# Retention and a mixture of experts on one core: up projections by seven half-size products instead of eight, sent between the down projections, with the attention as a chain of chunks

## The chip, the cores and the metric

One core of a Trainium2 chip. The metric is the device time of the core in microseconds (us), the median of several executions. The names in the profile: PE is the tensor engine's matmuls, PEld its weight loads, DVE VectorE, ACT ScalarE, POOL GpSimd, SP SyncE; "PEq" or "SPq" is the sequencer of an engine, where DMAs are issued. "PEclk" is the clock granted to PE, in tenths of full speed; "half clock" below means that the record of it reads 0.5.

## The reference

```python
def _attn_ref(q, k, v):                       # (8, 8, 576, 64): batches, heads, tokens, width
    scores = scale * np.matmul(q, k.transpose(0, 1, 3, 2))
    gamma = 1.0 - 2.0 ** (-5.0 - np.arange(H))            # one decay per head
    Dmat = np.where(rel >= 0, gamma[:, None, None] ** rel[None], 0.0)   # causal, rel = i - j
    return np.matmul(scores * Dmat[None], v)

def _moe_ref(x, domain_probs, w1, w2):        # x (4608, 512), w1 (4, 512, 1024), w2 (4, 1024, 512)
    p = domain_probs / (domain_probs.sum(-1, keepdims=True) + 1e-09)
    for e in range(E):
        h = np.maximum(x @ w1[e], 0.0)        # up projection
        out += p[:, e:e + 1] * (h @ w2[e])    # down projection
    return out
```

The attention's output, heads side by side, is the `x` of the mixture. The 4608 tokens are worked on in 9 tiles of 512, and each tile meets all four experts: 36 pairs of tile and expert.

## The kernel before

Attention and mixture run in one program. While tile t is multiplied, batch t+1's attention is slipped in between the groups of matmuls. The decay is split into a gain on k and a gain on q; whole chunks of 128 tokens leave a state (k transposed times v) behind for the chunks after them. A batch has 576 tokens: four chunks and a remainder of 64. The parts that matter here:

```python
# one pair: 32 up matmuls of 512 columns, ReLU on ACT, then 32 down matmuls
def up(ph, e, fc, ts):
    for dc in range(NDC):                                             # NDC = 4
        nc.tensor.matmul(ph[:, ts], lhsT=w1_sb[e][:, dc, fc * 128:(fc + 1) * 128],
                         rhs=xT[:, dc, n0 + ts.start:n0 + ts.stop], start=(dc == 0), stop=(dc == NDC - 1))
# ups(e): for fc in range(8): up(...); nc.scalar.activation(hT[:, fc, :], ph, Relu); yield
# downs(e): for ns in range(4): 8 matmuls into po, then
#           acc = po * p (ACT, first expert) or acc += po * p (DVE); the last expert stores acc
# ... (cut)
# batches 2 to 7: what goes in after which group of the tile before (32 up and 16 down groups)
at(19 if nt == 1 else 17, lambda: state["A"].S([0, 1]))               # scores of two head pairs
at(24, lambda: state["A"].Srem(), lambda: state["A"].O_values([0, 1]),
   lambda: state["A"].kv_all(), lambda: state["A"].kv_sum(), lambda: state["A"].Srem_mask())
at(28, lambda: state["A"].O_states([0, 1]))
at(30, lambda: state["A"].S([2, 3]))
at(34, lambda: state["A"].O_values([2, 3], rem=True), lambda: state["A"].O_states([2, 3], rem=True))
```

The score matmuls use 64 rows of the array (two heads side by side), the value and kv matmuls 64 columns; the state matmuls and all projections use the full 128x128 array. Tile 0 and the first part of tile 1 ("the head" below) run with batches 0 and 1, whose q and k are transposed by PE; from batch 2 on the DMA transposes.

## Time and profile before

| | before |
|---|---|
| time, median | 561.0 us (560.97 to 561.14 in the first three runs) |
| span of the profiled run, granted clock | 557.7 us, 0.999 |
| PE busy | 546.5 us |
| DVE, ACT, POOL busy | 166.9, 217.5, 118.6 us |

The page of the kernel before: busy time of each engine with its share of the span, then busy tenths in 40 slices of the span.

```profile
span 557.7 us, 8401 instructions
## 1 busy us (share of the span) xinstructions
PE 546.5 (98%) x3462; PEld 261.4 (47%) x3462; DVE 166.9 (30%) x288; ACT 217.5 (39%) x371; POOL 118.6 (21%) x203
...
PE   7999999899999999999999999999999999999997
...
PEclk9999999999999999999999999999999999999999
```

The chain of work that ended last, in order of time (start, length, what):

```profile
139.20 6.91 PE po L552 x32
146.11 6.91 PE ph L518 x32
153.01 6.91 PE po L552 x32
```

32 matmuls of 512 columns in 6.91 us are 216 ns each, one behind the other. The timeline of PE shows the head's landmarks (start, length, operation, output<-inputs, tile, count); the later comparison rests on these starts. The first line is the first up projection, the second batch 1's first scores, the third and fourth the start of tile 1's first up projections and the transposes of batch 1's remainder within them, and the last the first down projection of tile 1, where the head ends.

```profile
17.88 0.61 PE L518 MATMUL ph<-xT,wt 128*128 128x256 bf16 x4
...
65.92 0.40 PE L319 MATMUL s<-qkT 64*128 64x128 bf16 x8
...
83.13 2.77 PE L518 MATMUL ph<-xT,wt 128*128 128x384 bf16 x20
85.83 0.29 PE L266 MATMUL ptr<-ident,qrb 64*128 64x64 bf16 x4
...
90.85 7.07 PE L552 MATMUL po<-wt,hT 128*128 128x512 bf16 x32
```

And this is one piece of attention, 16 score matmuls, between projections:

```profile
239.62 1.89 PE L518 MATMUL ph<-xT,wt 128*128 128x512 bf16 x8
241.44 0.62 PE L286 MATMUL s<-qkT 64*128 64x128 bf16 x16
241.99 1.04 PE L518 MATMUL ph<-xT,wt 128*128 128x512 bf16 x4
```

How much PE time such a piece takes is read from starts: the 8 projections before it would be followed at 239.62 + 8 x 0.216 = 241.35 by the next one; it came at 241.99; so the piece cost 0.64 us (its median over the trace is 0.649). "The cost of a piece" below always means this.

### The profile page before, as it was taken

Reading aid. Unit: us, or ns where it says so; the run is one execution under the profiler, and the core shown is the slowest. Engines: PE = TensorE matmul, PEld = TensorE weight load, DVE = VectorE, ACT = ScalarE, POOL = GpSimd, SP = SyncE. Lnnn points to the kernel's source line nnn. Section 1 sums busy time; section 2 is a strip of 40 time slices with the busy share of each in tenths; the row PEclk is TensorE's granted clock in tenths of the full one; section 3 lists DMA queues with packets and bytes.
Section 4 is the critical chain, followed back from the end, with each engine's and each line's share of the span. In section 5 each row is a group of like instructions: output and inputs, shape, how many; then the busy total and the mean of one; then the engine's idle time right before and its main releaser. Section 6 shows DMA issues by size and latency. Waiting matters only on the chain.

```text
span 557.7 us, 8401 instructions
## 1 busy us (share of the span) xinstructions
PE 546.5 (98%) x3462; PEld 261.4 (47%) x3462; DVE 166.9 (30%) x288; ACT 217.5 (39%) x371; POOL 118.6 (21%) x203
## 2 busy tenths in 40 slices
PE   7999999899999999999999999999999999999997
PEld 4544444354445444544445444544454444444443
DVE  5402461253214520462035212532046202220222
ACT  6543424333353235323433334323532353335332
POOL 7701366026002420045002600260010000000000
PEclk9999999999999999999999999999999999999999
DMA  8999999491369025910595048903200100010002
GB/s 232 182 206 200 200 204 238 99 212 22 113 121 182 1 85 95 220 19 38 114 177 88 1 132 149 136 1 104 58 2 0 76 0 1 0 76 0 1 0 76
DMA packets 148805, 53.83 MB, mean 97 GB/s; under 512 B 130684, under 2 KB 143228, under 8 KB 148768
## 3 DMA queue, kind: packets, MB, share of 16 engines
q1 hardware_dynamic: 141296, 44.79, 40.2%
q0 software_dynamic: 7328, 8.39, 8.9%
q8 instruction: 27, 0.44, 0.4%
q10 hardware_dynamic: 144, 0.13, 0.1%
q14 instruction: 10, 0.08, 0.1%
HBM read 45.16 MB, written 9.44 MB: 98 GB/s over the span
## 4 chain that ended last, share of the span: by engine, by line
PE 82%; DMA 11%; SPq 3%; POOL 3%; issue 1%; DVE 0%; POOLq 0%
PE po L552 40%; PE ph L518 37%; DMA raw_v<-in_v_dram 4%; DMA wt<-in_moe_w_dram 2%; DMA raw_vr<-in_v_dram 2%; SPq L278 1%; PE o L358 1%; PE s L286 1%; DMA raw_k<-in_k_dram 1%; DMA raw_q<-in_q_dram 1%; PE o L366 1%; POOL wt L125 1%; SPq L85 1%; DMA qkT<-km 0%; SPq L91 0%
## 5 line engine op out<-in xcount | busy, mean ns | idle before, releaser
L539 ACT ACTIVATE hT<-ph 128x512 bf16<-128x512 f32 x288 | 171.9, 598 | 275.4 <-PE ph L518 275.4
L518 PE MATMUL ph<-xT,wt 128*128 128x512 bf16 (+2 forms) x1172 | 260.0, 376 | 0.0
L552 PE MATMUL po<-wt,hT 128*128 128x512 bf16 (+1 forms) x1160 | 255.9, 378 | 0.0
L552 PEld LDWEIGHTS <-hT 128*128 128x128 bf16 x1160 | 112.5, 98 | 132.9 <-DMA wt<-in_moe_w_dram 0.3
L518 PEld LDWEIGHTS <-wt 128*128 128x128 bf16 x1172 | 111.9, 98 | 127.9
L558 DVE SCALAR_TENSOR_TENSOR acc<-po,probs,acc 128x512 f32<-128x512 f32 (+1 forms) x109 | 81.3, 746 | 229.1 <-PE po L552 221.9
L293 DVE TENSOR_TENSOR sT<-s,tri 128x512 bf16<-128x512 f32 x48 | 29.8, 684 | 115.6 <-PE s L286 115.6
L556 ACT ACTIVATE acc<-po,probs 128x512 f32<-128x512 f32 x36 | 24.8, 690 | 38.2 <-PE po L552 38.2
L272 POOL COPY kbd<-qkT 64x256 bf16<-64x256 bf16 x12 | 4.8, 398 | 129.7 <-DMA qkT<-krb 129.4
L407 POOL CAST sbd<-ksum 64x256 bf16<-64x256 f32 x36 | 14.3, 398 | 83.3 <-DVE ksum L412 74.0
L239 POOL TENSOR_TENSOR km<-raw_k,gk 128x512 bf16<-128x512 f32 x28 | 29.1, 1041 | 12.5 <-DMA raw_k<-in_k_dram 10.9
L241 POOL CAST vm<-raw_v 128x512 bf16<-128x512 f32 x28 | 17.1, 612 | 41.9 <-PE o L358 35.2
L241 POOL CAST qm<-raw_q 128x512 bf16<-128x512 f32 x28 | 17.0, 608 | 3.6 <-DMA raw_q<-in_q_dram 3.2
L378 DVE TENSOR_TENSOR xT<-o,gq 128x512 bf16<-128x512 f32 x24 | 15.5, 686 | 6.0 <-PE o L366 5.5
L244 POOL TENSOR_TENSOR krb<-raw_kr,gk 64x512 bf16<-64x512 f32 x8 | 8.3, 1036 | 19.0 <-DMA raw_kr<-in_k_dram 19.0
L286 PE MATMUL s<-qkT 64*128 64x128 bf16 x192 | 7.7, 218 | 2.3 <-DMA qkT<-km 2.3
L286 PEld LDWEIGHTS <-qkT 64*128 64x128 bf16 x192 | 5.4, 94 | 7.6 <-issue 5.1
L358 PE MATMUL o<-sT,vm 128*64 128x128 bf16 x192 | 7.6, 222 | 0.0
L248 POOL CAST vbd<-raw_vr 64x256 bf16<-64x256 f32 x16 | 6.4, 398 | 3.4 <-DMA raw_vr<-in_v_dram 3.0
L358 PEld LDWEIGHTS <-vm 128*64 128x64 bf16 x192 | 5.7, 109 | 2.9 <-issue 2.5
L366 PE MATMUL o<-qkT,sbd 128*128 128x128 bf16 x72 | 6.2, 220 | 0.1
L141 PE MATMUL warm_out<-kbd 128*128 128x512 bf16 x14 | 4.9, 500 | 1.3 <-DVE kbd L136 1.3
(97 smaller groups left out, 152.2 us busy)
## 6 DMA issues: line engine op xcount, KB each, us to landing
out_dram<-acc SPq DMA_DIRECT2D x35, 256.0 KB, 2.0
raw_k<-in_k_dram SPq DMA_DIRECT2D x32, 256.0 KB, 5.1
raw_q<-in_q_dram SPq DMA_DIRECT2D x32, 256.0 KB, 5.1
raw_v<-in_v_dram SPq DMA_DIRECT2D x32, 256.0 KB, 5.2
wt<-in_moe_w_dram POOLq DMA_DIRECT2D x6, 1024.0 KB, 25.8
wt<-in_moe_w_dram POOLq DMA_DIRECT2D x4, 512.0 KB, 7.3
raw_kr<-in_k_dram SPq DMA_DIRECT2D x8, 128.0 KB, 5.1
raw_qr<-in_q_dram SPq DMA_DIRECT2D x8, 128.0 KB, 5.0
```

The costliest lines, as they stand in the source:

```text
L239: eng.tensor_tensor(o, i, gk[:, c, :].unsqueeze(2).to_broadcast([128, H, D]), op=MULT)
L241: eng.tensor_copy(o, i)
L286: nc.tensor.matmul(s[j][:, c, :], lhsT=self.qkT[r, 1, p, cs], rhs=self.qkT[r, 0, p, cs], start=True, stop=True)
L293: nc.vector.tensor_tensor(st[:, j], s[j], tri[:, :].unsqueeze(1).to_broadcast([128, NCH, C]), op=MULT)
L358: nc.tensor.matmul(o[64 * j:64 * j + 64, c * C:(c + 1) * C], lhsT=self.m["v"][:, c, 2 * p + j, :], rhs=self.sT[p][:, j, c, :], start=(c == ...
L378: nc.vector.tensor_tensor(xT[:, p, b * S:b * S + SM], o, gq[:, p, 0:SM], op=MULT)
L407: eng.tensor_copy(sbd[r, n, :, r], src[r])
L518: nc.tensor.matmul(ph[:, ts], lhsT=w1_sb[e][:, dc, fc * 128:(fc + 1) * 128], rhs=xT[:, dc, n0 + ts.start:n0 + ts.stop], start=(dc == 0), s ...
L539: nc.scalar.activation(hT[:, fc, :], ph, Relu)
L552: nc.tensor.matmul(po, lhsT=hT[:, fc, ns * 128:(ns + 1) * 128], rhs=w2_sb[e][:, fc, d:d + w], start=(fc == 0), stop=(fc == NFC - 1))
L556: nc.scalar.activation(a, po, Copy, scale=pe)
L558: nc.vector.scalar_tensor_tensor(a, po, pe, a, op0=MULT, op1=ADD)
```

## The change

Strassen's scheme (in Winograd's form) computes a 2x2 block product with seven half-size products instead of eight. Applied to an up projection (1024x512 times 512x512), it needs 7 x 8 matmuls of 256 columns where there were 32 of 512. The price is sums: of blocks of the weights, once per expert (DVE, in the head), of blocks of x, once per tile (POOL), and of products in PSUM (ACT and DVE, each half pair: a pair is done in two halves of its 1024 hidden features). To hide these the products alternate with the *down* projection of the pair before, four down matmuls to each gap between products. The attention of batches 2 to 7 becomes a chain of small tasks, at most one PE task to a gap. The head, with tile 0 and the first pair of tile 1, stays classical: 31 of the 36 pairs are fast ones. Also, q gets its gain as it is cast (before: as the attention's output left PSUM).

The core of the diff, shortened and not in the order of the file (cuts marked with `# ...`):

```diff
+    def weight_sums(e):                      # 10 DVE operations and 2 late ones per expert
+        # ... t1 = a21 + a22; t2 = t1 - a11; copies of both to bf16; a12 - t2; late: a21 = a11 - a21
+    def token_sums(nt):                      # 6 POOL operations per tile, scratch t1, t2 from pool "tmp"
+        # ... b12 - b11, b22 - t1, b22 - b12, b21 - t2, and two copies to bf16
+    def up_fast(nt, e, g, gap, window):      # one half pair
+        product(P, lambda k: w[:, k, :HF], lambda k: x[:, k, t0], start=True)
+        nc.scalar.activation(Q, P, Copy)
+        product(R_, lambda k: s[:, 0, k], lambda k: T[:, 0, k], start=True)
+        nc.scalar.activation(m5, R_, Copy)
+        window("DVE")
+        gap()
+        product(P, lambda k: s[:, 1, k], lambda k: T[:, 1, k])
+        nc.vector.tensor_tensor(R_, P, m5, op=ADD)
+        # ... four more products; hT gets ReLU(Q), ReLU(R_), ReLU(P), and P + m5 (DVE, clamped by POOL)
+        # ... (cut)
+        def gap():
+            for _ in range(4):
+                f = next(fill)               # one down matmul of the pair before
+                if f:
+                    evacuations.append(f)
+            sums(nt + 1)
+            pool(nt, 2)                      # two POOL tasks of the chain
+            chain.emit("PE", nt)             # at most one PE task of the chain
+            chain.seen.update(chain.done)
+            chain.now += 1
+        # ... (cut)
+            # the chain of a batch: scores S, kv and outputs O of the chunks, then the remainder
+            Sc(0, 0, -1 if n else 0), kv(0, 0), Sc(1, 2, 0), O(0, 3, 0), kv(1, 4), Sc(2, 5, 1), O(1, 6, 0), kv(2, 7)
+            Sc(3, 8, 2), O(2, 9, 0), kv(3, 10)
+    # ... (cut)
+    at(48, narrow, lambda: [f() for f in token_sums(1)], lambda: [a1().cast_rem(n, nc.gpsimd) for n in "kqv"])
+    sums_at(1, 17)                           # weight sums of expert 1 from group 17 of the head on, and so on
+    sums_late(1, 22)
+    sums_at(0, 23)
+    sums_at(2, 33)
+    sums_late(2, 38)
+    sums_at(3, 48)
+    sums_late(3, 53)
 # ... (cut)
-    apool = ctx.enter_context(tc.tile_pool(name="apool", bufs=6))
+    apool = ctx.enter_context(tc.tile_pool(name="apool", bufs=NSUB))        # 4 accumulators
```

## The prediction

> **What bounds the kernel now.** The tensor engine. The page has PE busy 546.5 us of a 557.7 us span; the rest mostly goes by before the first projections. In the chain of work that ended last PE holds 82%, and from 107 us on it reads "32 matmuls, 6.91 us" again and again: 216 ns per 128x512 matmul, no gaps. A tile of 512 tokens (one down projection to the same one a tile later, 226.93 to 286.37 us) takes 59.4 us: 8 x 6.91 = 55.3 of projections and 4.2 of the next batch's attention. Other engines have room (the page: DVE 30%, ACT 39%, POOL 21%); the granted clock is 0.999 (cores view). Only fewer PE cycles can help.
>
> **What is removed.** 31 of the 36 pairs of tile and expert go from 32 up matmuls of 512 columns to 7 x 8 = 56 of 256 columns. The trace has such matmuls: in the last down projection twelve in a row, each with its weight load, take 1.47 us from first start to last end (timeline); the last one lasts 0.27, so 11 starts take 1.20 us, 109 ns each. The Trainium skill, "TensorE: Matmul & The Clock Gate", section "Wait — 56ns, not 53.3ns?", gives a fixed cost of about 2.5 ns per warm matmul; 109 and 216 agree. A weight load takes 98 ns (groups), so it still hides, barely. Per pair: 56 x 0.109 = 6.10 against 6.91, 0.80 us saved; x 31 = 25 us, all on the critical path.
>
> **What is added.** Per pair, DVE gets four additions of 128x512 (estimate 0.7 us each, from the mask's 0.684), ACT four copies (0.6, as the Relu) less two Relus, POOL two clamps. Per tile, POOL gets six token sums and q's gain multiplication (1.04 us where the cast took 0.61). Estimated DVE load is 31 us of a 56 us tile, POOL 28: neither becomes the bound. The weight sums (48 DVE operations) fall into the first tile, beside evacuations with slack. Attention's matmuls stay, one piece per gap.
>
> **New waits.** Banks P, Q, R are reused within a half pair of about 6.5 us. Laid out with these durations each reuse has slack but one: the last product's Relu has four down matmuls (0.86 us, plus one matmul's 0.11) until P is written again, and needs about 0.27 + 0.6 + two semaphore steps = 1.0 us. I allow 0.05 us x 62 = 3 us. The attention chain may reach tile 2 late: 1 us, about what the old waits for transposes (2.3 us, groups) give back. The head stays within 1 us.
>
> **Sum.** 561 - 25 + 3 = 539 us. Range 532 to 547. Faster by over 2% (under 549.8): 0.92; within 2%: 0.07; slower: 0.01.
>
> **What would show it.** PE busy about 521 us; 256-column matmuls 109 ns apart inside a product; a tile period near 56.3 us; PE idle under 3 us in the fast part, ended by ACT's last Relu; DVE 45 to 50% busy; no wait for tokens at a tile's start.
>
> **What would make it wrong.** Weight loads that no longer hide: 20 ns x 1736 would cost 35 us and cancel the gain. PSUM-to-PSUM copies much slower than 0.6 us would make the P, Q, R chain PE's bound. Late tokens would show as PE idle of several us at tile starts. Output stores held up behind transposes could stall ACT, as only four accumulators are left.

The 109 ns in it were read from this line of the timeline of the kernel before, twelve matmuls of 256 columns in the last down projection:

```profile
552.64 1.47 PE L552 MATMUL po<-wt,hT 128*128 128x256 bf16 x12
```

## The result

| | before | changed |
|---|---|---|
| time, median | 560.99 us | 559.62 us (558.53 to 560.90) |
| ratio, 95% interval | | 0.9969 (0.9948 to 0.9990) |
| span of the profiled run, clock | 557.7 us, 0.999 | 558.7 us, 0.988 |
| PE busy | 546.5 us | 535.0 us |

A ratio is the mean time of a kernel's fast runs over that of the kernel before in the same rounds, so it isn't quite the ratio of the medians. The kernel before has a spread of its own: over all experiments, its 15 runs with a mean clock of 0.999 or 1.0 took 559.8 us on average, its 24 with 0.996 or 0.997 took 561.3, and 5 with 0.994 took 562.5. The traced execution is one of the first kind, so a comparison of the traces favours the kernel before by more than 1 us against the medians. The change is "the same" within 2%: 1.7 us gained where 22 were predicted. The page after:

```profile
span 558.7 us, 10485 instructions
## 1 busy us (share of the span) xinstructions
PE 535.0 (96%) x4133; PEld 334.5 (60%) x4206; DVE 266.3 (48%) x427; ACT 251.6 (45%) x450; POOL 225.9 (40%) x321
...
PE   8999876799999999999999999999999999999997
...
PEclk9999979799999999999999999999999999999999
```

PE is 11.5 us less busy, as it should be to some extent, yet the span is longer: PE is idle in slices 5 to 8 (56 to 112 us), and the granted clock drops there.

**Where the gain is.** A half pair without attention, on PE's timeline of the changed kernel (before: 13.82 / 2 = 6.91 us):

```profile
318.12 0.60 PE L583 MATMUL upP<-xT,wt 128*128 128x256 bf16 x4
318.55 0.60 PE L583 MATMUL upR<-tsum,wsum 128*128 128x256 bf16 x4
318.99 1.03 PE L519 MATMUL po<-wt,hT 128*128 128x512 bf16 x4
...
324.63 0.60 PE L583 MATMUL upP<-xT,wt 128*128 128x256 bf16 x4
```

From start to start 6.51 us: 28 x 0.109 + 16 x 0.216. Products follow each other 0.43 us apart, 4 matmuls of 109 ns. The fast matmuls do what was predicted: 31 pairs x (56 x 0.1095 - 32 x 0.2159) = -24.1 us.

**Where it went, first half: the head.** The same landmarks as before, on the changed kernel's PE timeline; a bracket is idle time of PE, with what ended it:

```profile
19.76 0.61 PE L478 MATMUL ph<-xT,wt 128*128 128x256 bf16 x4
...
72.73 0.61 PE L315 MATMUL s<-qkT 64*128 64x128 bf16 x8 [4.75 <-DVE qkT L298]
...
90.84 2.77 PE L478 MATMUL ph<-xT,wt 128*128 128x384 bf16 x20
100.42 0.39 PE L306 MATMUL ptr<-ident,qrb 64*128 64x64 bf16 x4 [6.80 <-POOL qrb L275]
...
108.37 0.60 PE L583 MATMUL upP<-xT,wt 128*128 128x256 bf16 x4
```

| landmark, start in us | before | changed | behind |
|---|---|---|---|
| first up projection | 17.88 | 19.76 | 1.9 |
| batch 1's first scores | 65.92 | 72.73 | 6.8 |
| tile 1's first up projections | 83.13 | 90.84 | 7.7 |
| transposes of batch 1's remainder | 85.83 | 100.42 | 14.6 |
| end of the head | 90.85 | 108.37 | 17.5 |

The head loses 17.5 us, 11.55 of them in two waits. The stretches-of-time view gives a mean clock of 0.89 from 60 to 91 us and 0.80 from 91 to 108.4 us: in each wait a stretch of 6.8 us at half clock begins (71.07 to 77.89 and 98.38 to 105.20 us in the clock record), in which 512-column matmuls start 427 ns apart. Of the two, 5.2 and 4.8 us lie after the wait's end; half of that, 5.0 us, is an estimate of what they cost. With the waits and the later start that is 18.4 us; less a wait of 0.92 us that only the kernel before has there (for POOL, at 71.9 us), it comes to the 17.5 lost. The Trainium skill, "TensorE: Matmul & The Clock Gate", section "HAM oscillation — how this bites in real kernels", says that an idle gap of more than some 3.4 us sends the clock to half; the trace agrees (waits of 4.75 and 6.80 us), but shorter waits did so in other runs (see the last section).

The first wait is for a copy on DVE. Its queue, on DVE's timeline of the changed kernel:

```profile
50.89 0.41 DVE L553 CAST wsum<-tmp 128x512 bf16<-128x512 f32 x1
...
68.22 1.26 DVE L553 CAST wsum<-tmp 128x512 bf16<-128x512 f32 x1
69.40 0.41 DVE L554 CAST wsum<-tmp 128x512 bf16<-128x512 f32 x1
...
70.34 2.01 DVE L556 TENSOR_TENSOR wt<-wt 128x512 bf16<-128x512 bf16 x2
72.27 0.41 DVE L298 COPY qkT<-ptc 128x512 bf16<-128x512 bf16 x1
```

On POOL's timeline:

```profile
67.72 1.48 POOL L267 TENSOR_TENSOR km<-raw_k,gk 128x512 bf16<-128x512 f32 x1
```

Expert 2's weight sums stand ahead of the copy, and they are slow there: such a cast takes 0.41 us at 50.89 and at 69.40, when POOL is idle, and 1.26 us at 68.22, when POOL multiplies k by its gain until 69.20. The Trainium skill, "SBUF — State Buffer", section "SBUF: two separate sides", has DVE and POOL share a port pair as an exclusive lock; the slow cast agrees with it, but no run here separates this from the order of the queue. The second wait is for a cast on POOL that stands behind six token sums (91.55 to 97.88), which could only start when batch 1's last tokens were there:

```profile
91.55 1.15 POOL L566 TENSOR_TENSOR tmp<-xT 128x512 f32<-128x512 bf16 x1 [15.69 <-DVE xT L233]
...
97.88 1.04 POOL L275 TENSOR_TENSOR krb<-raw_kr,gk 64x512 bf16<-64x512 f32 x1
98.88 1.48 POOL L275 TENSOR_TENSOR qrb<-raw_qr,gq 64x512 bf16<-64x512 f32 x1
```

**Second half: the attention in pieces.** A piece of 8 score matmuls in the changed kernel:

```profile
300.24 1.03 PE L519 MATMUL po<-wt,hT 128*128 128x512 bf16 x4
301.19 0.40 PE L315 MATMUL s<-qkT 64*128 64x128 bf16 x8
301.52 0.61 PE L583 MATMUL upP<-tsum,wt 128*128 128x256 bf16 x4
```

It costs 301.52 - (300.24 + 4 x 0.216) = 0.42 us, where 16 cost 0.65 before. So 8 matmuls are 0.22 us, and every piece has 0.20 us on top. Over all pieces of batches 2 to 7:

| | before | changed |
|---|---|---|
| pieces, and cost in all | 30, 27.8 us (2.5 of it waiting for a transpose) | 84, 36.0 us |
| score piece, median | 0.649 (16 matmuls) | 0.425 (8) |
| kv piece | with the value piece | 0.341 (8) |
| output piece with states | 1.242 (with the remainder) | 0.674 |
| remainder's scores, full array | with the value piece | 0.116 (4 of 64 columns) |

The remainder's scores, which use the full array, have no such surcharge: 256 columns in all for 0.116 us, where one 256-column matmul takes 0.109. The surcharge goes with the tiling: the kernel before has 24 pieces with smaller tiles in these batches, the changed one 72, and 48 x 0.217 us (the surcharge that the experiments give) is 10.4 us, where the costs differ by 36.0 - (27.8 - 2.5) = 10.7. The Trainium skill, "TensorEngine Tiling (Array Packing)", section "Key Properties", says that changing the tiling mode drains the tensor engine, without a figure. I had not looked at this page before predicting.

From the end of the head to the last down projection the kernel before takes 547.02 - 90.85 = 456.2 us. In the changed one it starts after the four down matmuls of the last gap, which begin at 547.13, so at 548.0, and 439.6 us have passed: 16.5 us gained, which is 24.1 for the products less 8.2 for the pieces, within 0.6. With 17.5 lost in the head this makes the 1.0 us by which the changed span is longer. (The medians have it 1.4 us shorter: the traced execution of the kernel before is some 1.5 us under the span of its median run, that of the changed kernel 0.8 us above.)

### The profile page after: what moved, and what is told of

It is laid out like the page before. It is cut to its first block, busy times and chain, and to the rows that moved or that the text cites. A ratio compares the mean times of both kernels' runs of the same rounds, so it can differ in the third digit from the quotient of the medians.

```text
span 558.7 us, 10485 instructions
## 1 busy us (share of the span) xinstructions
PE 535.0 (96%) x4133; PEld 334.5 (60%) x4206; DVE 266.3 (48%) x427; ACT 251.6 (45%) x450; POOL 225.9 (40%) x321
## 4 chain that ended last, share of the span: by engine, by line
PE 91%; DVE 5%; issue 1%; POOL 1%; DMA 1%; SPq 0%; POOLq 0%; DVEq 0%
PE po L519 43%; PE upP L583 20%; PE upR L583 10%; PE ph L478 5%; PE upQ L583 5%; PE oc L356 2%; PE s L315 2%; PE kvp L326 1%; PE oc L359 1%; DVE wt L556 1%; DMA raw_q<-in_q_dram 1%; DVE wsum L555 0%; PE warm_out L153 0%; DVE acc L509 0%; DVE xT L233 0%
## 5 line engine op out<-in xcount | busy, mean ns | idle before, releaser
L604 POOL TENSOR_SCALAR hT<-hT 128x512 bf16<-128x512 bf16 x62 | 38.1, 614 | 211.5 <-DVE hT L603 210.7
L595 DVE TENSOR_TENSOR upR<-upP,m 128x512 f32<-128x512 f32 x62 | 43.4, 699 | 126.9 <-PE upP L583 126.9
L583 PEld LDWEIGHTS <-wsum 128*128 128x128 bf16 x744 | 72.6, 98 | 21.1
L583 PE MATMUL upP<-tsum,wt 128*128 128x256 bf16 x496 | 74.8, 273 | 0.1
L603 DVE TENSOR_TENSOR hT<-upP,m 128x512 bf16<-128x512 f32 x62 | 42.9, 692 | 55.7 <-PE upP L583 54.2
L494 ACT ACTIVATE hT<-ph 128x512 bf16<-128x512 f32 x40 | 23.5, 597 | 41.6 <-PE ph L478 40.8
L478 PE MATMUL ph<-xT,wt 128*128 128x512 bf16 (+3 forms) x174 | 39.7, 377 | 0.6 <-issue 0.4
L583 PE MATMUL upP<-xT,wt 128*128 128x256 bf16 x248 | 37.4, 273 | 0.0
L583 PE MATMUL upQ<-xT,wt 128*128 128x256 bf16 x248 | 37.2, 273 | 0.0
L583 PE MATMUL upP<-tsum,wsum 128*128 128x256 bf16 x248 | 37.2, 273 | 0.0
```

Of the source, the lines that this page charges most:

```text
L583: nc.tensor.matmul(ps[:, l], lhsT=wa(kc)[:, f:f + 128], rhs=xa(kc), start=(start and l == 0 and kc == 0), stop=(kc == 1), skip_group_check ...
L595: nc.vector.tensor_tensor(R_, P, m5, op=ADD)
L603: nc.vector.tensor_tensor(h22, P, m5, op=ADD)
L604: nc.gpsimd.tensor_scalar(h22, h22, float("inf"), 0.0, op0=MIN, op1=MAX)
```

## The experiments

My theory was thus: the products bring their 24 us; the head's waits (called Q, for queue order, in the expectations) and changes of tiling (D) take it back. Rivals: the fast part doesn't deliver and the head doesn't matter (F); POOL's own slowness makes the waits (P); the cost of a piece belongs to each insertion, whatever its tiling (G). "Against the changed kernel" below is the difference of the two ratios to the kernel before, times 561 us, as the calls need not have run on the same chip.

### e1_sums_early: weight sums where DVE idles

```diff
-    sums_at(1, 17)
+    sums_at(1, 17, 10)
     sums_late(1, 22)
-    sums_at(0, 23)
-    sums_at(2, 33)
-    sums_late(2, 38)
+    sums_at(0, 18, 10)
+    sums_at(2, 23)
+    sums_late(2, 34)
```

> The changed kernel with the weight sums of experts 1, 0 and 2 put earlier in VectorE's program (into its idle stretch at 29 to 43 us), so that none stands ahead of the q and k copies of batch 1. Theory Q (queue order: the 4.75 us wait of the score matmuls at 68 us is a copy queued behind weight sums on VectorE): that wait goes, and so does the half-clock stretch after it; 5 to 7 us faster than the changed kernel, near 553.5; the 6.8 us wait of the remainder's transposes on POOL stays. Rival F (the fast part's 256-column matmuls do not deliver and the head does not matter): within 1 us of 559.6. Rival P (the copy is late because POOL's casts are late): the wait stays above 3 us.

552.51 us, ratio 0.9847 (0.9819 to 0.9875): 6.8 us less than the changed kernel. The wait for the copy is gone, one half-clock stretch is left of two, and the 6.80 us wait stays. Theory Q holds for the first wait; F and P fall for it.

### e2_rem_early: the remainder's casts ahead of the token sums

```diff
-    at(48, narrow, lambda: [f() for f in token_sums(1)], lambda: [a1().cast_rem(n, nc.gpsimd) for n in "kqv"])
+    at(48, narrow, lambda: [f() for f in token_sums(1)])
+    at(44, lambda: [a1().cast_rem(n, nc.gpsimd) for n in "kqv"])
```

> The changed kernel with batch 1's remainder casts on POOL put ahead of the six token sums instead of behind them. Theory Q: the transposes no longer wait (6.8 us gone there), but their copies on VectorE stand behind the weight sums of expert 3, which wait for the token sums' scratch buffers, so most of the wait moves to the remainder's score matmuls: a new PE wait of 3 to 6 us on VectorE's copy, and only 1 to 4 us faster than the changed kernel, 556 to 558. Rival P (POOL's order alone): 7 us or more faster, below 553.

559.36 us, ratio 0.9976 (0.9941 to 1.0011): no gain. The list of PE's waits has this in the place of the one removed:

```profile
PE sr L368 <- DVE kbd L290: 6.4, 1, 6.4
```

The wait moved on almost whole (6.4 of 6.8 us) to the next matmuls, whose operands DVE copies behind expert 3's weight sums, and those wait for the scratch buffers that the token sums hold, 2.79 and 2.73 us on DVE's timeline. The second of these waits:

```profile
97.02 1.52 DVE L550 TENSOR_TENSOR tmp<-tmp,wt 128x512 f32<-128x512 f32 x1 [2.73 <-POOL tsum L568]
```

The mechanism was as expected; the 1 to 4 us weren't there.

### e3_both: both, and expert 3's sums spread over the fast part

```diff
-    sums_at(3, 48)
-    sums_late(3, 53)
+    spread, late[3] = weight_sums(3)         # after the head
+    spread += late[3]
 # in gap():
+            if spread:
+                spread.pop(0)()
```

> Both moves, and expert 3's weight sums spread one per gap over the first fast pairs. Theory Q: PE's two waits in the head go (11.5 us), and with them the two half-clock stretches (estimate 3 to 4 us, from 21 matmuls of 512 columns at 427 instead of 216 ns): 543 to 547. What remains to the 539 predicted is then the attention's smaller pieces (estimate 8 us). Rival F: above 556.

550.69 us, ratio 0.9811 (0.9783 to 0.9839): 8.9 us less than the changed kernel, where 13 to 17 were expected. Both waits are gone and the head ends at 91.44 us, but twelve matmuls later stands a new one, in which a half-clock stretch begins:

```profile
98.58 0.61 PE L315 MATMUL s<-qkT 64*128 64x128 bf16 x8 [5.24 <-DMA qkT<-km]
```

It is the transpose of batch 2's first chunk. In the changed kernel PE had been late enough not to meet it.

### e4_dup: one product computed twice

```diff
         product(P, lambda k: w[:, k, :HF], lambda k: x[:, k, t0], start=True)
+        product(P, lambda k: w[:, k, :HF], lambda k: x[:, k, t0], start=True)
```

> The changed kernel with the first product of each half pair computed twice (the second start overwrites the first, the result stays right): 62 x 4 more 256-column matmuls. If PE's stream bounds the fast part and such a matmul costs 109 ns, 27 us slower than the changed kernel, 586.5 (585 to 589). If instead the chain P, Q, R through ACT and VectorE bounds it, PE has room and it costs under 10 us, below 570; if weight loads did not hide, over 32 us.

585.47 us, ratio 1.0446 (1.0407 to 1.0486), results right: 26.8 us more than the changed kernel for 62 x 4 matmuls, 108 ns each. The fast part is bound by PE's stream, and a 256-column matmul costs what the trace of before said. The chain through P, Q and R does not bound it, and the weight loads hide.

### e5_pair and e6_pair_sf: fewer pieces, and fewer changes of tiling

e5_pair sends each kv piece in one gap with the output piece before it:

```diff
-            chain.emit("PE", nt)
+            if chain.emit("PE", nt) and chain.done["PE"] % 14 in (4, 7, 10):
+                chain.emit("PE", nt, strict=False)
 # O(0, 3, 0), O(1, 6, 0), O(2, 9, 0) become O(0, 4, 0), O(1, 7, 0), O(2, 10, 0)
```

e6_pair_sf also puts the state matmuls of an output piece, which use the full array, ahead of its value matmuls:

```diff
+            for p in range(NP if c else 0):
+                nc.tensor.matmul(o[:, p, :], lhsT=sbd[:, c - 1, p, :], rhs=self.qc(0, c)[:, p],
+                                 start=(p == 0), stop=False, skip_group_check=True)
             # ... value matmuls, start=(c == 0 and p == 0)
-            # ... the state matmuls stood here
```

> The changed kernel, with each kv piece of the attention sent in the same gap as the output piece before it (18 times), so 66 insertions into the projections instead of 84; the output piece still ends with its full-array state matmuls, so for 12 of the 18 the array's tiling changes as often as before. Theory D (each change into 64-row or 64-column tiles and back costs about 0.2 us, a drain): the 12 pairs cost as much as the two pieces alone (0.674 + 0.341 = 1.0 us each), only the 6 pairs without state matmuls save 0.2 us; about 1.2 us in all, near 558.4. Rival G (each insertion costs, whatever the tiling): 18 x 0.2 = 3.6 us.

> As the run before it in this list, and the state matmuls (full array) come first in the output piece, so that its tiled part and the kv piece are neighbours. Theory D: all 18 pairs now cost about 0.2 us less than the two pieces alone (0.8 instead of 1.0 us), 3.6 us in all, near 556. Rival G: the same as the run before it.

Median costs in the two traces: a pair with states takes 1.015 us in e5_pair (0.674 + 0.341, to the last digit the two alone) and 0.787 in e6_pair_sf, where an output piece with the states first costs 0.663 alone; a pair without states, the first chunk's, takes 0.564 in both, against 0.440 + 0.341 alone. So a pair saves 0.217 us (0.663 + 0.341 - 0.787 and 0.440 + 0.341 - 0.564) exactly where it saves a change of tiling, and nothing elsewhere: theory D holds for the pieces, and G falls. But the times were 565.26 us (ratio 1.0088, 1.0059 to 1.0118) and 564.11 us (1.0065, 1.0036 to 1.0094), 5 to 7 us *more* than the changed kernel. That expectation failed. In both PE waits anew for ACT: in e6_pair_sf 6.9 us in two waits, the longer of 5.5 us (in e5_pair 6.0 and 4.9), in which a third half-clock stretch begins. On PE and, just before, on ACT in e6_pair_sf:

```profile
182.03 1.01 PE L584 MATMUL upP<-tsum,wsum 128*128 128x256 bf16 x4 [5.47 <-ACT upQ L590]
```

```profile
180.80 0.69 ACT L508 ACTIVATE acc<-po,probs 128x512 f32<-128x512 f32 x1 [6.64 <-DMA out_dram<-acc]
```

ACT waits for an accumulator whose store to memory is late; SyncE issues stores in one queue with transposes and loads. In the changed kernel the same wait is 1.86 us, and PE doesn't feel it.

### e12_pair_store: the same with stores out of SyncE's queue

```diff
-                eng.dma_start(out=out[t * 128:(t + 1) * 128, cols], in_=a)
+                stores.append(store)          # ACT issues it at the next evacuation, when acc is long done
```

> e6_pair_sf with the output stores taken out of SyncE's queue. e6_pair_sf was slower than the changed kernel although its attention took 4 us less, and I put that to ACT waiting 6.6 us for an accumulator whose store stood behind transposes. If so: the 6.9 us wait of PE for ACT goes, and the run is 3 to 4 us faster than the changed kernel, 555 to 557. If the wait was something else, it stays above 562.

554.78 us, ratio 0.9888 (0.9866 to 0.9910): 4.5 us less than the changed kernel. PE's wait for ACT is gone, the two waits of the head are as they were. So the store was the cause, and 18 saved changes are worth their 18 x 0.217 = 3.9 us, within the noise.

### e8_before_split and e13_split_scores: the kernel before with more pieces

e13 halves the score pieces; e8 does that and puts kv_all and kv_sum one group after O_values.

```diff
-            at(19 if nt == 1 else 17, lambda: state["A"].S([0, 1]))
+            at(19 if nt == 1 else 17, lambda: state["A"].S([0]))
+            at(20 if nt == 1 else 18, lambda: state["A"].S([1]))
 # and S([2, 3]) at 30 becomes S([2]) at 30 and S([3]) at 31
 # e8 alone: kv_all, kv_sum at 25 instead of at 24
```

> The kernel before, with its attention cut into smaller pieces: score matmuls of one head pair per insertion instead of two (12 more tiled pieces in the six batches), and the kv matmuls one group later than the value matmuls instead of next to them (6 more). Same matmuls, no Strassen products. Theory D: each more change of tiling costs about 0.2 us wherever it happens: 18 x 0.2 = 3.6 us slower than the kernel before, +0.6%, and in the trace an 8-matmul score piece takes 0.425 us as in the changed kernel, where the 16-matmul one took 0.649. Rival: the cost belongs to the changed kernel's gaps (semaphores, short products); then within 1 us of the kernel before.

> The kernel before, with only the score matmuls cut in two: 12 more tiled pieces in the six batches, the kv matmuls left where they were. Theory D: 12 x 0.217 = 2.6 us slower than the kernel before, +0.5% (0.3 to 0.7%), and no new wait of PE over 1 us. e8_before_split was 8.6 us slower, of which its trace gives 4 us to waits for POOL's state copies that my moving the kv matmuls had made, not to drains.

e8 took 569.79 us, ratio 1.0153 (1.0140 to 1.0166), 8.6 us more. That is more than twice what I expected. The pieces themselves are as expected (score piece 0.426 us; the two halves of the cut group 0.780 + 0.721, together 0.217 more than the 1.284 before), but the states now came late and PE waited 4.0 us for POOL's copies, in six waits; that was my edit. The clean cut, e13, took 563.68 us, ratio 1.0046 (1.0031 to 1.0062): 2.6 us more, as predicted from 12 x 0.217. So a change of tiling costs the same without any of the new scheme.

### e9_casts_early and e7_best: two runs with wrong results

Both cast batch 2's first chunks on POOL before the token sums; e7_best has e6_pair_sf's pairs too.

```diff
-    for g in range(49, 56):
+    for g in [45, 46, 47] + list(range(49, 56)):
         at(g, lambda: pool(1, 2))
```

> As e3_both, and POOL casts the first two chunks of batch 2 before the token sums of the second tile instead of behind them. Theory Q: the 5.2 us wait for the transposes, which e3_both had in the place of the two removed waits, goes with its half-clock stretch: 5.2 + about 1.5 us faster than e3_both's 550.7, 543 to 545. If another wait appears in the head, the gain is under 3 us.

> e9_casts_early and e6_pair_sf together. If waits in the head and drains add up: 3.6 us faster than e9_casts_early, 539 to 542, the time that was predicted for the change (539), and over 3% faster than the kernel before.

Their results were wrong (relative error 0.07), by my mistake: six tasks more before the end of the head let batch 2's remainder overwrite vbd and kbd, which hold the remainder's values and keys, while batch 1 still needed them. The times (554.05 and 559.64 us; PE waited 9 to 10 us for the overtaking cast of vbd) say nothing about the theories.

### e10_head_store and e11_all: the same made right

```diff
-    for g in [45, 46, 47] + list(range(49, 56)):
+    for g in (45, 46, 47, 52, 53, 54, 55):
 # and the stores as in e12_pair_store; e11_all has the pairs too
```

> e9_casts_early made right (POOL's early work limited so that it doesn't overtake batch 1's remainder) and the output stores of the fast part issued by ACT one step later, so that they no longer stand behind transposes in SyncE's queue. Theory Q: no PE wait over 2 us is left in the head; 5.2 us of wait and about 1.5 us of half clock less than e3_both (550.7): 543 to 546.

> e10_head_store with the output and kv pieces paired, state matmuls first. If the drains saved add to it: 3.6 us faster than e10_head_store, 539.5 to 542.5; the pairs must not bring back the wait of ACT for output stores that e6_pair_sf had (6.6 us).

549.22 us (ratio 0.9789, 0.9775 to 0.9804) and 545.73 us (0.9727, 0.9712 to 0.9742). The pairs save 3.5 us, as expected, and e11_all is the first that is over 2% faster than the kernel before beyond its interval (e10_head_store's reaches 0.9804). But e10_head_store missed its 543 to 546: the wait for batch 2's transposes is still there, 4.5 us (5.2 in e11_all), though the casts were early. What was late is the issue. SyncE's timeline in e11_all:

```profile
83.47 1.11 SPq L109 DMA_DIRECT2D raw_k<-in_k_dram  x1
84.62 1.09 SPq L109 DMA_DIRECT2D raw_q<-in_q_dram  x1
...
91.93 1.32 SPq L284 DMA_TRANSPOSE qkT<-qm  x1
```

Each load holds SyncE for about 1.1 us, from 72 to 90 us without a pause, and the transposes come after them in its program.

### e15_head_later and e14_all_later: the first scores five gaps later

```diff
-                        ok = (b, c) in self.begun and (not strict or self.now >= self.begun[b, c] + 5)
+                        ok = (b, c) in self.begun and (not strict or self.now >= self.begun[b, c] + (13 if (b, c) == (2, 0) else 5))
```

> e10_head_store, with the first score piece of batch 2 held back five gaps (about 8 us), so that it comes after its transposes, which SyncE issues only at 92 us because its queue is full of loads until then. If that was the last wait of the head: 4.5 us of wait and half of 6.8 us at half clock go, 7.9 us in all, and it takes 541.3 (540 to 543). If the chain of the attention gets late by it, PE waits at the second tile and the gain is under 3 us.

> e11_all with the same score piece held back: 5.2 us of wait and 3.4 us of half clock less than 545.7: 537 (535.5 to 539), 3.6 to 4 us under e15_head_later through the 18 saved changes of tiling. It would be 4.2% faster than the kernel before, the gain that the products alone were predicted to give.

545.01 us (ratio 0.9733, 0.9708 to 0.9759) and 545.23 us (0.9715, 0.9692 to 0.9738). The transposes' wait is gone, but both missed: a fourth wait came, 3.1 and 2.9 us. In e14_all_later, on PE and on POOL:

```profile
117.26 1.03 PE L528 MATMUL po<-wt,hT 128*128 128x512 bf16 x2 [2.86 <-POOL hT L613]
```

```profile
115.65 0.85 POOL L290 COPY kbd<-qkTr 64x256 bf16<-64x256 bf16 x2 [13.99 <-DMA qkTr<-krb]
116.59 0.61 POOL L613 TENSOR_SCALAR hT<-hT 128x512 bf16<-128x512 bf16 x1
```

The clamp of hT stood behind a copy that waited 14 us for another transpose that SyncE had issued late. The two kernels differ by the pairs, which were expected to save 3.6 to 4 us; the ratios differ by 1.0 us, and the intervals overlap (the runs spread over 4 us), so these two runs neither show nor refute that saving.

### e16_krem_later: that copy eight gaps later

```diff
-    (13 if (b, c) == (2, 0) else 5)
+    {(2, 0): 13, (2, NCH): 13}.get((b, c), 5)
```

> e14_all_later, with POOL's copy of batch 2's remainder keys put eight gaps later in POOL's program. In e14_all_later that copy held POOL for 14.0 us (waiting for a transpose that SyncE issues only at 113 us), the clamp of hT stood behind it, and the down projection waited 2.9 us for the clamp. If that was the last wait of the fast part's start, it goes: 2 to 4 us less than e14_all_later's 545.2, 541 to 543, with PE's only wait over 1.5 us in the trace gone and the clock at half nowhere after 20 us. If a further wait appears, it is within 1 us of 545.

540.67 us, ratio 0.9636 (0.9613 to 0.9658), results right: 4.4 us less than e14_all_later by the ratios (its range had 2 to 4), and 20.4 us less than the kernel before. Its page:

```profile
span 538.8 us, 10541 instructions
## 1 busy us (share of the span) xinstructions
PE 529.3 (98%) x4206; PEld 334.3 (62%) x4206; DVE 258.6 (48%) x427; ACT 251.3 (47%) x450; POOL 222.7 (41%) x321
...
PEclk9999999999999999999999999999999999999999
```

PE's longest wait is 1.3 us, at the start; the head ends at 90.23 us (90.85 in the kernel before) and has no half-clock stretch; the 66 insertions cost 31.2 us. All of the products' gain is there but for the pieces, which still cost more than before (31.2 against 27.8 us).

## Why the prediction was wrong

The prediction was 539 us (532 to 547), 92% for faster by over 2%; measured were 559.62.

- **Right: the bound and the products.** "Per pair ... 0.80 us saved; x 31 = 25 us, all on the critical path": 24.1 in the trace (0.78 per pair), and 26.8 us for doubling one product (e4_dup). Weight loads hide: 109.5 ns.
- **Right, with too much allowed: the P, Q, R chain.** 3 us were set aside for the last ReLU; PE doesn't wait for it in the changed kernel.
- **Wrong, the step that failed first: "The weight sums (48 DVE operations) fall into the first tile, beside evacuations with slack", and "The head stays within 1 us".** The head lost 17.5 us. I had checked that DVE has time on average; what counts is what stands ahead of what in its queue. One batch's copies, which PE needs at once, stood behind weight sums on DVE, and the remainder's casts behind token sums on POOL, and the two are also tied by shared scratch buffers (e2_rem_early). In each wait a stretch of 6.8 us at half clock began. Shown by e1_sums_early (one wait, 6.8 us) and by the sequence up to e16_krem_later.
- **Wrong: "Attention's matmuls stay, one piece per gap", taken as free.** The matmuls are the same, but 84 insertions instead of 30 cost 36.0 us instead of 27.8, 0.217 us for each change into a smaller tiling and back. Shown on the traces of e5_pair and e6_pair_sf, on time by e11_all (3.5 us against e10_head_store; e14_all_later against e15_head_later did not show it), and in the kernel before by e13_split_scores (2.6 us).
- **Seen, and not given a size: "Output stores held up behind transposes could stall ACT".** It does nothing in the changed kernel, but it cost e6_pair_sf over 5 us, and e12_pair_store removed it.
- **What was to show it:** DVE came out 48% busy, as predicted (45 to 50); PE busy was 535 us instead of 521, for the half clock and the pieces; a tile took 57.8 us on average (56.0 to 61.9, tiles 2 to 6) instead of 56.3. "The attention chain may reach tile 2 late" did not happen; PE meets no wait for tokens at a tile's start.

Why no single repair gave the gain back: behind each wait stood another resource that was just as late. Removing the DVE wait left POOL's; removing both left the transposes, late for SyncE's issue; then POOL behind a late transpose. With all four gone and 18 changes of tiling saved, the kernel takes 540.7 us, close to the 539 predicted for the change as it stood. That the two agree to 2 us is partly luck: the 3 us set aside for the ReLU were not used, and the pieces still cost 3.4 us more than before.

Open: how much of the slow DVE sums is POOL's share of the port and how much comes from the longer queue alone; and the 1.9 us by which the changed kernel starts its first projections later (19.76 against 17.88 us; 18.97 in e16_krem_later), which no run isolates.

## What to carry to other kernels

When a change trades tensor work for small operations on other engines, check for each operation that the tensor engine will wait for what stands ahead of it in its engine's queue, not how busy that engine is; and take waits away together, since the next one often stands right behind. Count the changes of the array's tiling: at 0.2 us each, many small tiled pieces between full-array matmuls cost more than a few large ones. A wait of a few us costs more than itself if the clock falls to half in it.

## What the Trainium skill lacked or had wrong

- "TensorEngine Tiling (Array Packing)", "Key Properties", says that changing the tiling mode drains the engine and gives no figure. Here it is 0.217 us for going from the full array to 64-row or 64-column tiles and back (e5_pair, e6_pair_sf, e8_before_split).
- "TensorE: Matmul & The Clock Gate", section "Back-to-back issue gap", gives about 131 ns as the sustained spacing of 512-column matmuls with a weight load each. Here it is 216 ns (6.91 us for 32), which is the same page's formula for the isolated gap; 256 columns take 109 ns.
- The same page, section "HAM oscillation — how this bites in real kernels", puts the idle gap that sends the clock to half at more than some 3.4 us. Here stretches at half clock also began in waits of 3.1 us (e15_head_later, 6.8 us at half), 2.9 (e14_all_later, 3.4 us) and 2.3 (e8_before_split and e13_split_scores, 3.4 us), while the same wait of 2.3 us in the trace of the kernel before had none. Most stretches lasted 6.8 us in the clock record, of which 3.5 to 6.1 us came after work was back.
- "DMA: Bandwidth & Descriptors", section "Issuing engines are not separate DMA queues", calls the sequencer's time to start a DMA usually small next to the DMA. Here one load of 256 KB held SyncE for about 1.1 us of the 4.8 to 5.1 us (medians) from issue to landing, one transpose for 1.2 to 2.0 us where 2.5 is the median to landing, and 18 us of loads stood ahead of the transpose that PE waited for (e11_all).
- "SBUF — State Buffer" describes the lock between DVE and POOL and names two slowdowns without the operations they belong to; it has no time for a DVE cast beside a POOL operation. Here a 128x512 cast on DVE took 0.41 us alone and 1.26 beside a 1.48 us multiplication on POOL (the changed kernel).
